# A list scheduler inside the kernel sets every engine's order in a fused window attention and feed-forward kernel, with chunk 1's attention ahead of most weight slices

## The chip, the core and the metric

The kernel runs on one core of a Trainium2 chip. The metric is device time in microseconds (us) of one execution; the kernel before takes 979.98 us, the median of three runs (979.28 to 980.83). The core has five engines that run their own instruction streams in order and wait for each other through semaphores: TensorE (PE; PEld is its weight load), VectorE (DVE), ScalarE (ACT), GpSimd (POOL) and SyncE (SP, which here only issues DMAs).

## What is computed

Windowed causal attention (a query sees itself and the 63 positions before it), then a feed-forward layer with mish, all in float32:

```python
B, H, S, D = 8, 8, 576, 64
scores = q @ k.T / sqrt(D)
mask = (rel >= 0) & (rel < 64)            # rel = query position - key position
attn = exp(scores - max); attn /= sum(attn) + 1e-9
x = (attn @ v).transpose(0, 2, 1, 3).reshape(4608, 512)
h = x @ w_in                               # w_in 512 x 2048
g = h * tanh(log1p(exp(h)))
out = g @ w_out                            # w_out 2048 x 512
```

## The kernel before

The 4608 tokens are cut into 12 chunks (c) of 384. The attention of a chunk is four *units*, one for each pair of heads (p). A unit loads q_t, k_t and v_t; PE makes the scores of six blocks of 64 queries against 128 keys (s_ps, 24 matmuls); DVE reduces each 128x128 piece (L149: adds the mask, gives the row's extreme), ACT takes the exponential (L152), DVE normalises (L156 to L158 in halves for chunk 0, L160 to L162 whole otherwise). The result pr has to be turned: for chunks 0 to 3 PE transposes it into t_ps (L183) and ACT or DVE copies it to pT (L184); for later chunks DVE transposes 32x32 blocks (L172) and twelve small DMAs move them (L177). PE then multiplies with v (o_ps, 24 matmuls), and the sum is split into a high part xh (ACT, L204) and a low part xl (DVE, L205), which only together carry float32.

The feed-forward part runs in *steps* (c, f): 16 slices f of the weights for each chunk. ffn_in makes h_ps from x with 12 matmuls of 128x384 (L213, recorded at helper line L95); ACT applies mish (L220) and the result t is split into gh (ACT for chunk 0, L222; POOL otherwise, L224) and gl (POOL, L225). ffn_out adds nine matmuls of 128x512 into three accumulators acc, two steps later (LAG).

The weights come as 64-bit floats, 1 MB a slice, and load_w turns each slice into a high and a low half once, during the first chunk: ACT clears the sign (L261), DVE does two short operations (L262, L264) and two long ones (L265, L266), ACT rounds (L270), DVE subtracts (L271). The tile wa has two buffers; the load of slice f waits until L266 of slice f-3 is done.

What sets the order: tiles come from pools, and the framework's own scheduler orders each engine's instructions by a simulated time line and priorities (`tc.high_priority`); only from chunk 2 on PE's matmuls are tied into one chain (in_order). The sequence of steps is written out: chunk 0's attention first, the steps (0, f) for f below 8 (HEAD), then (0, f) and (1, f-8) by turns, then the rest of chunk 1, then chunk after chunk. The attention of chunk 1 is planned into the first eight steps (`atts[1].plan`), that of chunk 2 into the last of chunk 1, and every later one over the steps of the chunk before, with four steps between scores and values. The accumulators of chunk 1 use the attention banks (tag "at"), so they can only start when its attention is done.

Of the kernel before, what the change touches and what calls it, by code (L numbers as in the profile page):

```python
# [26 lines left out]
@with_exitstack
def tile_window_attn_mish_ffn(
# [65 lines left out]
    def pe(*args, **kw):
        order.append(nc.tensor.matmul(*args, **kw).ins)  # L95
# [11 lines left out]
    def load_qk(c, p):  # L110
        q_t = ap_.tile([P, CH], F32, name="q_t")
        k_t = ap_.tile([P, CH + BLK], F32, name="k_t", bufs=2)
        parts = NM if c == 0 and p < 1 else 1
        for i in range(parts):
# [4 lines left out]
        return q_t, k_t

    def load_v(c, p):

        v_t = ap_.tile([P, NB, P], F32, name="v_t", bufs=2)
        src = vN[p, c * CH:, :]
        nc.sync.dma_start(v_t, bass.AP(tensor=vN.tensor, offset=src.offset,
                                       ap=[[P, P], [BLK * P, NB], [1, P]]))
        return v_t

    def att_scores(c, p, tiles):
        q_t, k_t = tiles  # L130
        s_ps = [bank(c, p, "s_ps").rearrange("p (m k) -> p m k", k=P) for _ in range(2)]
        pr = ap_.tile([P, HM, P], F32, name="pr", bufs=2)
        mx = ap_.tile([P, HM], F32, name="mx", bufs=3)
        sm = ap_.tile([P, HM], F32, name="sm", bufs=3)
        for m in range(NM):
            for par, h in ((0, 0), (1, 1), (1, 0), (0, 1)):
                n = 2 * m + par
                rows = slice(h * BLK, (h + 1) * BLK)
                pe(s_ps[h][par * BLK:(par + 1) * BLK, m, :],
                   q_t[rows, n * BLK:(n + 1) * BLK], k_t[rows, n * BLK:n * BLK + P],  # L140
                                 start=True, stop=True)
        for h in range(2):
            js = slice(h * NM, (h + 1) * NM)
            for m in range(NM):
                first = [(c * NB + 2 * m + par) % blocks_per_seq == 0 for par in range(2)]
                mk = firsts[first.index(True)] if any(first) else mask
                j = h * NM + m

                nc.vector.tensor_tensor_reduce(  # L149
                    out=pr[:, j, :], in0=s_ps[h][:, m, :], in1=mk,  # L150
                    op0=ALU.add, op1=ALU.min, scale=-0.125, scalar=3.0e38, accum_out=mx[:, j:j + 1])
                nc.scalar.activation(pr[:, j, :], pr[:, j, :], AF.Exp, bias=mx[:, j:j + 1], scale=-1.0,  # L152
                                     accum_out=sm[:, j:j + 1])
            if c == 0:

                nc.vector.tensor_scalar(sm[:, js], sm[:, js], 1e-9, None, ALU.add)  # L156
                nc.vector.reciprocal(sm[:, js], sm[:, js])
                nc.vector.tensor_tensor(pr[:, js, :], pr[:, js, :], sm[:, js].unsqueeze(2).to_broadcast([P, NM, P]), ALU.mult)  # L158
        if c > 0:
            nc.vector.tensor_scalar(sm, sm, 1e-9, None, ALU.add)  # L160
            nc.vector.reciprocal(sm, sm)
            nc.vector.tensor_tensor(pr, pr, sm.unsqueeze(2).to_broadcast([P, HM, P]), ALU.mult)  # L162
        return pr

    def att_transpose(c, p, pr):
        pT = next(pTs)
        if c > 3:


            moved = []  # L170
            tr = ap_.tile([P, P // 32, HM, 32], F32, name="tr", tag="pr", bufs=2)
            nc.vector.transpose(tr.rearrange("p k j i -> p j k i"),  # L172
                                pr.rearrange("p j (k i) -> p j k i", i=32))
            for r in range(0, P, 32):
                for k in range(0, P, 32):
                    if 0 <= k - r % BLK <= BLK:
                        moved.append(nc.sync.dma_start(pT[k:k + 32, r // 32, :, :], tr[r:r + 32, k // 32, :, :]))  # L177
            return pT, moved
        for h in range(2):
            t_ps = (bank(c, p, "t_ps") if c else ps_h.tile([P, CH], F32, name="t_ps", tag="h_ps")  # L180
                    ).rearrange("p (m k) -> p m k", k=P)
            for m in range(NM):
                nc.tensor.transpose(t_ps[:, m, :], pr[:, h * NM + m, :], ident)  # L183
            (nc.scalar.copy if h == 0 or c == 1 else nc.vector.tensor_copy)(  # L184
                pT[:, :, h * NM:(h + 1) * NM, :].rearrange("p r m i -> p m r i"),
                t_ps.rearrange("p m (r i) -> p m r i", i=32))
        return pT, []

    def att_values(c, p, v_t, pT, x):
        pT, moved = pT  # L190
        xh, xl = x
        o_ps = bank(c, p, "o_ps")
        for n in range(NB):
            m, par = n // 2, n % 2
            for h in range(2):
                rows = slice(h * BLK, (h + 1) * BLK)
                pe(o_ps[rows, n * BLK:(n + 1) * BLK], v_t[:, n, rows],
                   pT[:, 2 * par:2 * par + 2, h * NM + m, :], start=True, stop=True)

                for d in moved:  # L200
                    tc.add_manual_dep(order[-1], d.ins.name, SYNC, reason="values in one piece")
                moved = []
        with tc.high_priority(offset=SOON):
            nc.scalar.copy(xh[:, p, :], o_ps)  # L204
            nc.vector.tensor_tensor(xl[:, p, :], o_ps, xh[:, p, :].bitcast(F32), ALU.subtract)  # L205

    def ffn_in(c, x, f):
        xh, xl = x
        h_ps = ps_h.tile([P, CH], F32, name="h_ps", tag="h_ps")
        n = 0  # L210
        for cc in range(NC_):
            for part, xx in ((0, xh), (0, xl), (1, xh)):
                pe(h_ps, ws[f][:, 0, part, cc * P:(cc + 1) * P], xx[:, cc, :],  # L213
                   start=n == 0, stop=n == 3 * NC_ - 1)
                n += 1
        t = mp.tile([P, CH], F32, name="t", tag="t", bufs=4)
        gh = mp.tile([P, CH], F32R, name="gh", bufs=3)
        gl = mp.tile([P, CH], F32R, name="gl", bufs=3)
        with tc.high_priority(offset=SOON):
            nc.scalar.activation(t, h_ps, AF.Mish)  # L220
# [212 lines left out]
```

## Time and profile before

| | |
|---|---|
| median of 3 runs | 979.98 us |
| the profiled execution, its own time | 979.27 us |
| its span, first to last instruction | 977.5 us |
| mean granted TensorE clock | 0.976 |
| start of chunk 2's first step (timeline of PE) | 229.18 us |
| accumulating matmuls from 966.90 us, last of PE | 5.74 us |
| last output store issued (instructions of tile o) | 974.2 us |

The profiled execution is 0.7 us below the median. All times inside it count from the span's start. The granted clock is the share of its full speed that TensorE's clock was given in a stretch. A wait is put down to the engine and line that released it last.

### The profile page before, as it was taken

The numbers are of one execution on the slowest core, as the hardware profiler recorded it, in microseconds if no ns is written. First come the engines' busy times: TensorE is split into PE (matmuls) and PEld (weight loads), VectorE is DVE, ScalarE is ACT, GpSimd is POOL, SyncE is SP. The second block draws the span as 40 slices with busy tenths as digits, with TensorE's granted clock in tenths as the row PEclk, the third lists the DMA queues.
The fourth block names the chain that finished last, engine by engine and source line by source line (L and its number), as shares of the span: only waits on it lengthen the run. The fifth ranks groups of instructions, "written<-read, shape, count | busy, mean of one in ns | idle before, by whom it ended". The sixth has DMA issues, their size and how long they took to land.

```text
span 977.5 us, 16844 instructions
## 1 busy us (share of the span) xinstructions
PE 929.9 (95%) x6432; PEld 821.7 (84%) x6432; DVE 276.3 (28%) x916; ACT 417.8 (43%) x1004; POOL 292.8 (30%) x385
## 2 busy tenths in 40 slices
PE   4698599998999999999999999999999999999998
PEld 2586399887888898888889888898888889889997
DVE  6988800122231321221221221221221221220000
ACT  5689511553553533533533443443443353451111
POOL 1023033231223233333333333333323323323332
PEclk9599699998999999999999999999999999999999
DMA  9655200122121311311311312322222221210000
GB/s 312 229 193 199 95 1 1 50 68 83 52 68 47 113 53 53 113 51 54 112 51 55 110 51 56 101 60 56 90 71 56 85 78 54 84 30 13 33 1 33
DMA packets 78033, 76.09 MB, mean 78 GB/s; under 512 B 9344, under 2 KB 71296, under 8 KB 75904
## 3 DMA queue, kind: packets, MB, share of 16 engines
q1 hardware_dynamic: 77952, 75.01, 24.5%
q8 instruction: 51, 0.84, 0.4%
q14 instruction: 30, 0.25, 0.1%
HBM read 56.10 MB, written 9.44 MB: 67 GB/s over the span
## 4 chain that ended last, share of the span: by engine, by line
PE 87%; DVE 7%; ACT 3%; issue 1%; DMA 1%; SPq 1%; ACTq 0%
PE h_ps L95 40%; PE acc L95 39%; PE o_ps L95 4%; PE s_ps L95 4%; DVE w L271 1%; DVE wa L265 1%; DVE wa L266 1%; DMA st<-w 1%; DVE wa L262 1%; DVE wa L264 1%; ACT wa L261 1%; ACT pr L152 1%; DVE pr L149 1%; PE t_ps L183 1%; ACT L220 1%
## 5 line engine op out<-in xcount | busy, mean ns | idle before, releaser
L95 PE MATMUL h_ps<-xh,w 128*128 128x384 f32 x1536 | 431.1, 341 | 3.7 <-ACT xh L204 2.7
L95 PE MATMUL acc<-w,gh 128*128 128x512 f32 x1152 | 363.5, 397 | 1.5 <-ACT gh L222 1.5
L95 PEld LDWEIGHTS h_ps<-xh,w 128*128 128x128 f32 x1536 | 284.2, 190 | 13.9 <-ACT xh L204 3.3
L220 ACT ACTIVATE t<-h_ps 128x384 f32<-128x384 f32 x192 | 94.0, 491 | 440.4 <-PE h_ps L95 439.7
L95 PE MATMUL h_ps<-xl,w 128*128 128x384 f32 x768 | 260.8, 340 | 2.9 <-DVE xl L205 2.9
L224 POOL TENSOR_SCALAR gh<-t 128x384 fp32r<-128x384 f32 x176 | 90.3, 513 | 568.6 <-ACT t L220 566.1
L95 PEld LDWEIGHTS acc<-w,gh 128*128 128x128 f32 x1152 | 211.9, 188 | 39.7 <-issue 6.3
L225 POOL TENSOR_TENSOR gl<-t,gh 128x384 fp32r<-128x384 f32 x192 | 198.4, 1034 | 106.9 <-ACT gh L222 92.2
L95 PE MATMUL acc<-w,gl 128*128 128x512 f32 x576 | 224.5, 391 | 0.6 <-POOL gl L225 0.6
L95 PEld LDWEIGHTS h_ps<-xl,w 128*128 128x128 f32 x768 | 145.8, 190 | 11.5 <-DVE xl L205 3.9
L205 DVE TENSOR_TENSOR xl<-o_ps,xh 128x384 fp32r<-128x384 f32 x48 | 26.7, 556 | 379.4 <-ACT xh L204 379.4
L95 PEld LDWEIGHTS acc<-w,gl 128*128 128x128 f32 x576 | 108.2, 188 | 25.1 <-POOL gl L225 1.0
L152 ACT ACTIVATE pr<-pr,mx 128x128 f32<-128x128 f32 x288 | 112.1, 391 | 14.8 <-DVE mx L149 14.3
L149 DVE CUSTOM_DVE_ANT_0 pr<-s_ps,mask 128x128 f32<-128x128 f32 x288 | 64.6, 285 | 30.8 <-PE s_ps L95 30.8
L220 ACT ACT_TABLE_LOAD x48 | 61.6, 1283 | 12.7 <-PE h_ps L95 12.4
L152 ACT ACT_TABLE_LOAD x42 | 53.9, 1283 | 28.9 <-DVE mx L149 28.7
L95 PEld LDWEIGHTS o_ps<-pT,v_t 128*64 128x64 f32 x1152 | 43.7, 150 | 24.3 <-issue 11.2
L95 PE MATMUL o_ps<-pT,v_t 128*64 128x64 f32 x1152 | 51.9, 240 | 9.8 <-DVE pT L184 4.7
L95 PE MATMUL s_ps<-k_t,q_t 64*64 64x128 f32 x1152 | 50.8, 293 | 4.0 <-DMA k_t<-kT 4.0
L152 ACT ACTIVATION_READ_ACCUMULATOR pr<-pr,mx 128x1 f32 x288 | 54.0, 187 | 0.0
L243 DVE COPY o<-acc 128x512 f32<-128x512 f32 x12 | 8.3, 692 | 149.2 <-PE acc L95 148.8
L95 PEld LDWEIGHTS s_ps<-k_t,q_t 64*64 64x64 f32 x1152 | 36.1, 140 | 11.3 <-DMA q_t<-qT 3.9
(36 smaller groups left out, 343.9 us busy)
## 6 DMA issues: line engine op xcount, KB each, us to landing
v_t<-vN SPq DMA_DIRECT2D x48, 384.0 KB, 3.7
st<-w SPq DMA_DIRECT2D x16, 1024.0 KB, 5.1
k_t<-kT SPq DMA_DIRECT2D x47, 224.0 KB, 3.8
out<-o SPq DMA_DIRECT2D x36, 256.0 KB, 2.1
pT<-tr SPq DMA_DIRECT2D x384, 24.0 KB, 1.8
q_t<-qT SPq DMA_DIRECT2D x47, 192.0 KB, 3.7
q_t<-qT SPq DMA_DIRECT2D x3, 64.0 KB, 2.0
k_t<-kT SPq DMA_DIRECT2D x2, 64.0 KB, 2.1
```

What stands on the lines that cost most here:

```text
L95: order.append(nc.tensor.matmul(*args, **kw).ins)
L149: nc.vector.tensor_tensor_reduce(out=pr[:, j, :], in0=s_ps[h][:, m, :], in1=mk, op0=ALU.add, op1=ALU.min, scale=-0.125, scalar=3.0e38, acc ...
L152: nc.scalar.activation(pr[:, j, :], pr[:, j, :], AF.Exp, bias=mx[:, j:j + 1], scale=-1.0, accum_out=sm[:, j:j + 1])
L183: nc.tensor.transpose(t_ps[:, m, :], pr[:, h * NM + m, :], ident)
L205: nc.vector.tensor_tensor(xl[:, p, :], o_ps, xh[:, p, :].bitcast(F32), ALU.subtract)
L220: nc.scalar.activation(t, h_ps, AF.Mish)
L224: nc.gpsimd.tensor_scalar(gh, t, 1.0, 0.0, ALU.mult, ALU.add)
L225: nc.gpsimd.tensor_tensor(gl, t, gh.bitcast(F32), ALU.subtract)
L261: nc.scalar.activation(af, hi.bitcast(F32), AF.Abs)
L262: nc.vector.tensor_scalar(af, af, BIG, TINY, ALU.min, ALU.max)
L264: nc.vector.tensor_scalar(a, a, 3, 0x3FFFFFFF, ALU.logical_shift_left, ALU.bitwise_and)
L265: nc.vector.scalar_tensor_tensor(a, hi, 0xC0000000, a, ALU.bitwise_and, ALU.bitwise_or)
```

## The change

The scheduler of the framework is switched off (`tc.manual_schedule()`), and the kernel brings its own. Every piece of work is a Task on one engine with a cost from a table, the buffers that it reads and writes, and a rank. Plan.order walks through time: the engine that can start first takes, among its tasks that are ready at that moment, the one of lowest rank, where an ACT task that needs another function table counts 20 ranks later. The tasks are then emitted sorted by planned start, so each engine's instructions stand in the program in that order. Tiles are fixed rings and the eight PSUM banks are named: A (three, acc), B (three, at), H (two, h).

With it come these moves:

- Ranks: units 0 to 3 have 0 to 6, units 4 to 7 (chunk 1) 22, 32, 34 and 36; slices 0 to 3 have 15, 18, 20 and 30, the later ones 40 to 95. Loads of a slice wait for slice f-2 instead of f-3.
- Chunk 1's steps follow chunk 0's at a distance of five slices (TRAIL) and alternate with them, instead of eight.
- gl of chunks 0 and 1 is made by DVE, gh by ACT; POOL does both from chunk 2 on.
- The sign of slices 6 and up is cleared on DVE instead of ACT.
- Chunk 3 is turned by DVE and DMAs, not by PE.
- Unit 0's q and k are loaded whole, and its k from ACT's queue. Chunk 1's pT copies go both to ACT; of the three stores of a chunk DVE does two.

```diff
+    def order(self):
...
+        for _ in self.tasks:
+            at, e = min((max(free[e], min(r for r, _ in ready[e])), e) for e in ready if ready[e])
+
+            def key(rt):
+                r, t = rt
+                switch = t.table not in (None, table)
+                return t.rank + SWITCH * switch, t.n
+
+            now = [rt for rt in ready[e] if rt[0] <= at + 1e-6]
+            pick = min(now, key=key)
...
+        return sorted(self.tasks, key=lambda t: (t.start, t.n))
...
+    ctx.enter_context(tc.manual_schedule())
...
+        pace = used[f - 2:f - 1] if f > 1 else []
...
+        if on_act:
+            x = add("ACT", "abs", lambda: nc.scalar.activation(af, words[1].bitcast(F32), AF.Abs),
...
+        else:
+            x = add("DVE", "absv", lambda: nc.vector.tensor_scalar(a, words[1], 0x7FFFFFFF, None, ALU.bitwise_and),
...
+        queue = nc.scalar if c == 0 and p == 0 else nc.sync
+        add("SP", "issue", lambda: nc.sync.dma_start(q_t, qT[p, :, a:b]), writes=[u.q[1]], rank=rank, size=P * CH * 4)
+        add("SP", "issue", lambda: queue.dma_start(k_t, kT[p, :, a:b + BLK]), writes=[u.k[1]], rank=rank,
...
+        if c < 2:
+            add("ACT", "gh", lambda: nc.scalar.copy(gh, t), reads=[tb], writes=[ghb], rank=post)
+            add("DVE", "gl", lambda: nc.vector.tensor_tensor(gl, t, gh.bitcast(F32), ALU.subtract),
+                reads=[tb, ghb], writes=[glb], rank=post)
+        else:
+            add("POOL", "poolgh", lambda: nc.gpsimd.tensor_scalar(gh, t, 1.0, 0.0, ALU.mult, ALU.add),
...
+    RANK_U = [0, 2, 4, 6, 22, 32, 34, 36]
+    RANK_W = [15, 18, 20, 30] + [40 + 5 * i for i in range(12)]
...
+    seq = sorted([(f + TRAIL * c + 0.5 * c, c, f) for c in range(2) for f in range(NF)])
+    for n, (_, c, f) in enumerate(seq):
+        ffn_in(c, f, r_ffn(c, f), False, c == 0 and f < 2)
+        if n >= LAG:
+            late(*seq[n - LAG][1:])
...
+            at = (last - NF + 4 * p, last - NF + 4 * p + 4) if c > 3 else (3 + 5 * p // 2, 7 + 5 * p // 2)
```

Three places show what moved. The first is PE around the last two units of chunk 1. Before (xh_557 and xl_558 are chunk 1's, t_ps and o_ps the units'), after the last of chunk 0's steps whose slice is ready:

```order
L183 MATMUL t_ps<-ident,pr 128x128 x6
L95 MATMUL o_ps<-pT_102,v_t 64x64
L95 MATMUL s_ps<-k_t,q_t 64x128 x12
L95 MATMUL o_ps<-pT_102,v_t 64x64 x11
L95 MATMUL h_ps<-xh_557,w 128x384
L95 MATMUL h_ps<-xl_558,w 128x384
L95 MATMUL h_ps<-xh_557,w 128x384
L183 MATMUL t_ps<-ident,pr 128x128 x6
L95 MATMUL o_ps<-pT_103,v_t 64x64 x12
```

In the change (acc_124 to acc_126 are chunk 0's accumulators, the at banks hold the units):

```order
L384 MATMUL at_128<-pT_103,v_t_93 64x64 x12
L348 MATMUL at_129<-ident,pr_96 128x128 x3
L348 MATMUL at_127<-ident,pr_96 128x128 x3
L451 MATMUL acc_124<-w,gh_110 128x512 x2
L451 MATMUL acc_124<-w,gl_113 128x512
L451 MATMUL acc_125<-w,gh_110 128x512 x2
L451 MATMUL acc_125<-w,gl_113 128x512
L451 MATMUL acc_126<-w,gh_110 128x512 x2
L451 MATMUL acc_126<-w,gl_113 128x512
L384 MATMUL at_128<-pT_104,v_t_94 64x64 x12
```

Accumulating matmuls of slice 4 of chunk 0 now stand between the last unit's transposes and its values; before, some eight slices of chunk 0 were ahead of these rows, and nothing but pieces of chunk 1 stood among them.

The second place is DVE while the later slices are made. Before, the operations of two slices (wa has two buffers) follow each other:

```order
L271 TENSOR_TENSOR w<-wa,w 128x2x512
L264 TENSOR_SCALAR wa<-wa 128x1024
L265 SCALAR_TENSOR_TENSOR wa<-st,wa 128x1024
L262 TENSOR_SCALAR wa<-wa 128x1024
L266 SCALAR_TENSOR_TENSOR wa<-st,wa 128x1024
```

In the change (L246 clears the sign, L427 is gl):

```order
L246 TENSOR_SCALAR wa_119<-st 128x1024
L248 TENSOR_SCALAR wa_119<-wa_119 128x1024
L266 TENSOR_TENSOR w<-wa_118,w 128x2x512
L427 TENSOR_TENSOR gl_114<-t_105,gh_111 128x384
L249 TENSOR_SCALAR wa_119<-wa_119 128x1024
L427 TENSOR_TENSOR gl_112<-t_106,gh_109 128x384
L251 SCALAR_TENSOR_TENSOR wa_119<-st,wa_119 128x1024
```

The gl of two steps, which stood on POOL, now stand among the operations of a slice, and one short operation has come over from ACT.

The third place is PE where chunk 2's last unit leads into its first step. Before (acc_1 and acc_2 are chunk 1's accumulators, xh_1681 chunk 2's):

```order
L95 MATMUL acc_2_1110<-w,gh 128x512 x2
L95 MATMUL acc_2_1110<-w,gl 128x512
L95 MATMUL s_ps<-k_t,q_t 64x128 x6
L95 MATMUL o_ps<-pT_102,v_t 64x64 x12
L183 MATMUL t_ps<-ident,pr 128x128 x6
L95 MATMUL o_ps<-pT_103,v_t 64x64 x12
L95 MATMUL h_ps<-xh_1681,w 128x384
```

In the change (at_127 to at_129 are chunk 1's accumulators; the last scores stand just above):

```order
L451 MATMUL at_128<-w,gh_110 128x512 x2
L451 MATMUL at_128<-w,gl_113 128x512
L348 MATMUL acc_125<-ident,pr_95 128x128 x3
L451 MATMUL at_129<-w,gh_110 128x512 x2
L451 MATMUL at_129<-w,gl_113 128x512
L348 MATMUL acc_126<-ident,pr_95 128x128 x3
L384 MATMUL acc_124<-pT_103,v_t_93 64x64 x12
L348 MATMUL acc_125<-ident,pr_96 128x128 x3
L348 MATMUL acc_126<-ident,pr_96 128x128 x3
L384 MATMUL acc_124<-pT_104,v_t_94 64x64 x12
L409 MATMUL h_130<-xh_120,w 128x384
```

Between the last scores and that unit's transposes (pr_96) there stood only the values of the unit before; now nine accumulating matmuls, the transposes and the values of the unit before stand there.

More of the change, by code (lines that the diff above doesn't have):

```diff
@@ L121, in load_v @@
-    def load_v(c, p):
-        v_t = ap_.tile([P, NB, P], F32, name="v_t", bufs=2)
-        src = vN[p, c * CH:, :]
[L125 to L134, printed above, removed]
+    ident = const.tile([P, P], F32, name="ident")
@@ L135, in att_scores, with emit_scores @@
+    class Unit:
+        pass
+    def emit_scores(u):
         for m in range(NM):
@@ L138, in att_scores @@
                 rows = slice(h * BLK, (h + 1) * BLK)
-                pe(s_ps[h][par * BLK:(par + 1) * BLK, m, :],
-                   q_t[rows, n * BLK:(n + 1) * BLK], k_t[rows, n * BLK:n * BLK + P],
+                nc.tensor.matmul(u.s[h][0][par * BLK:(par + 1) * BLK, m * P:(m + 1) * P],
+                                 u.q[0][rows, n * BLK:(n + 1) * BLK], u.k[0][rows, n * BLK:n * BLK + P],
                                  start=True, stop=True)
-        for h in range(2):
[L143 to L178, printed above, removed]
-        for h in range(2):
[L180 to L187, printed above, removed]
@@ new lines, in turn_pe, with tr, copy @@
+    def turn_pe(u, rank, engines, chain):
+        pr, prb = u.pr
+        pr = pr.rearrange("p (j k) -> p j k", k=P)
+        pT, pTb = u.pT = pT_ring.take()
+        for h in range(2):
+            t_ps, tb = u.t[h]
+            def tr(h=h, t_ps=t_ps):
+                for m in range(NM):
+                    nc.tensor.transpose(t_ps[:, m * P:(m + 1) * P], pr[:, h * NM + m, :], ident)
+            add("PE", "tr", tr, reads=[prb], writes=[tb], after=[u.normed[h]], rank=rank, chain=chain)
+            def copy(h=h, t_ps=t_ps):
+                (nc.scalar.copy if engines[h] == "ACT" else nc.vector.tensor_copy)(
+                    pT[:, :, h * NM:(h + 1) * NM, :].rearrange("p r m i -> p m r i"),
+                    t_ps[:, :CH].rearrange("p (m r i) -> p m r i", m=NM, i=32))
+            add(engines[h], "pT", copy, reads=[tb], writes=[pTb], rank=rank)
+        u.moved = []
@@ L196, in att_values @@
                 rows = slice(h * BLK, (h + 1) * BLK)
[L197 to L205, printed above, removed]
@@ L395, in tile_window_attn_mish_ffn, with values @@
-    while pend:
-        with in_order():
-            flush()
+                mm = nc.tensor.matmul(o_ps[rows, n * BLK:(n + 1) * BLK], v_t[:, n, rows],
+                                      pT[:, 2 * par:2 * par + 2, h * NM + m, :], start=True, stop=True)
+                for d in u.moved:
+                    tc.add_manual_dep(mm.ins, d.ins.name, SYNC, reason="values in one piece")
+                u.moved = []
+    def values(u, rank, chain):
+        add("PE", "values", lambda: emit_values(u), reads=[u.v[1], u.pT[1]], writes=[u.o[1]], rank=rank, chain=chain)
@@ new lines, in tile_window_attn_mish_ffn, with bank, tail, front @@
+    rot = [0]
+    def bank(pool):
+        rot[0] += 1
+        return pool[(rot[0] - 1) % 3]
+    def tail(i):
+        u, r = units[i], RANK_U[i]
+        if i >= 4:
+            pool = B if i < 8 else A
+            u.t = [bank(pool), bank(pool)]
+            u.o = bank(pool)
+        turn_pe(u, r, ("ACT", "ACT") if 4 <= i < 8 else ("ACT", "DVE"), False)
+        values(u, r, False)
+        refill_v(i)
+        x_parts(u, r)
+    def front(i):
+        u, r = units[i], RANK_U[i]
+        if i >= 4:
+            pool = B if i < 8 else A
+            u.s = [bank(pool), bank(pool)]
+        scores(u, r, False)
+        refill_qk(i)
+        softmax(u, r, i < 4)
@@ new lines, in tile_window_attn_mish_ffn @@
+    for n, (c, f) in enumerate(steps):
+        r = 1000 + 10 * n
+        ffn_in(c, f, r, True, False)
+        for kind, i in sorted(runs.get(n, []), key=lambda x: x[0], reverse=True):
+            u = units[i]
+            if kind == "s":
+                u.s, u.o = B[:2], B[2]
+                scores(u, r, True)
+                refill_qk(i)
+                softmax(u, r - 4, False)
+                turn_dma(u, r - 4)
+            else:
+                values(u, r, True)
+                refill_v(i)
+                x_parts(u, r - 5)
+        if n >= LAG:
+            ffn_out(*steps[n - LAG], r + 15, True)
@@ L400 @@
+    for n in range(N - LAG, N):
+        ffn_out(*steps[n], 10000 + n, True)
+    tasks = plan.order()
+    if REPORT:
+        REPORT(tasks)
+    for t in tasks:
+        t.emit()
+REPORT = None
 def kernel(**inputs):
```

528 lines of the change are left out of this document (333 added, 195 removed).

## The prediction

> **What bounds the kernel now.** The page first: who is busy.
>
> ```profile
> PE 929.9 (95%) x6432; PEld 821.7 (84%) x6432; DVE 276.3 (28%) x916; ACT 417.8 (43%) x1004; POOL 292.8 (30%) x385
> ```
>
> PE fills the span on average, so the question is where it doesn't. Busy time by stretch (start:end, length, then PE, PEld, DVE, ACT, POOL, each with its count, granted clock, DMA share, GB/s):
>
> ```profile
> 0.00:25.00 25.00, 10.51 (x131) 7.21 (x131) 17.50 (x62) 13.83 (x40) 4.12 (x17) 0.94 0.90 311
> 25.00:50.00 25.00, 17.54 (x133) 13.52 (x133) 24.97 (x62) 16.82 (x43) 0.00 (x0) 0.58 0.69 232
> 50.00:75.00 25.00, 23.04 (x155) 20.03 (x154) 22.15 (x36) 22.13 (x37) 7.12 (x5) 1.00 0.57 202
> 75.00:100.00 25.00, 20.54 (x138) 17.11 (x137) 22.39 (x33) 22.05 (x37) 6.24 (x5) 1.00 0.47 167
> 100.00:125.00 25.00, 13.88 (x102) 10.95 (x103) 19.22 (x35) 13.91 (x28) 2.47 (x3) 0.66 0.29 92
> 125.00:150.00 25.00, 25.00 (x128) 22.78 (x127) 0.00 (x0) 4.48 (x9) 7.62 (x9) 1.00 0.00 1
> ```
>
> Up to 125 us PE is idle for 39.5 us and twice works at a low granted clock (0.58, 0.66), while DVE is busy 106.2 of 125. From 125 on PE is full. What PE waits for before 125 us (total, times, longest):
>
> ```profile
> PE t_ps L183 <- DVE pr L158: 7.7, 3, 3.2
> PE t_ps L183 <- DVE pr L162: 7.0, 3, 3.6
> PE o_ps L95 <- DVE pT L184: 4.7, 2, 2.8
> PE h_ps L95 <- DVE xl L205: 2.9, 3, 1.2
> ```
>
> DVE results, each time: the first 125 us are bound by DVE and by attention chains through it; everything later by PE alone. How much PE has to do at full rate comes from the chain of waits:
>
> ```profile
> 131.54 2.11 PE h_ps L95 x12
> ...
> 148.21 2.11 PE h_ps L95 x12
> ...
> 301.46 2.11 PE h_ps L95 x12
> ...
> 320.01 2.09 PE h_ps L95 x12
> ...
> 966.90 5.74 PE acc L95 x25
> ```
>
> 131.54 to 148.21 is four steps (a slice f for a chunk): 4.167 us each. 301.46 to 320.01 is four steps and one attention unit: 1.88 us a unit. A unit that PE transposes costs 0.60 us more, from one start to the next:
>
> ```profile
> 80.77 0.85 PE L183 MATMUL t_ps<-ident,pr 128*128 128x128 f32 x6 [0.22 <-DVE pr L162]
> 81.37 0.71 PE L95 MATMUL acc<-w,gh 128*128 128x512 f32 x2
> ```
>
> Before: 192 x 4.167 + 48 x 1.88 + 16 x 0.60 = 899.9 us. PE ends at 972.6, so it **loses 72.7 us**, nearly all before 125 us and at chunk 2's start. The change is worth what it cuts from those 72.7, plus 4 x 0.60 (chunk 3 goes to the DMA turn).
>
> **The change, part by part.** *Prices on DVE* (start to next start):
>
> ```profile
> 43.19 0.28 DVE L149 CUSTOM_DVE_ANT_0 pr<-s_ps,mask 128x128 f32<-128x128 f32 x1
> ...
> 43.40 0.29 DVE L149 CUSTOM_DVE_ANT_0 pr<-s_ps,mask 128x128 f32<-128x128 f32 x1
> ...
> 48.54 0.55 DVE L205 TENSOR_TENSOR xl<-o_ps,xh 128x384 fp32r<-128x384 f32 x1
> 49.00 1.22 DVE L266 SCALAR_TENSOR_TENSOR wa<-st,wa 128x1024 uint32<-128x1024 uint32 x1
> 50.14 0.69 DVE L262 TENSOR_SCALAR wa<-wa 128x1024 f32<-128x1024 f32 x1
> 50.74 0.18 DVE L161 RECIPROCAL sm<-sm 128x6 f32<-128x6 f32 x1
> 50.86 0.69 DVE L264 TENSOR_SCALAR wa<-wa 128x1024 uint32<-128x1024 uint32 x1
> 51.47 0.95 DVE L162 TENSOR_TENSOR pr<-pr,sm 128x768 f32<-128x768 f32 x1
> 52.34 1.22 DVE L271 TENSOR_TENSOR w<-wa,w 128x1024 fp32r<-128x1024 f32 x1
> 53.47 2.04 DVE L265 SCALAR_TENSOR_TENSOR wa<-st,wa 128x1024 uint32<-128x1024 uint32 x1
> ```
>
> A softmax reduction 0.21, a 128x384 operation 0.46, a long weight operation 1.14, a short one 0.60, a full norm 0.87; a pair on sm about 0.4 (estimate from two of 0.18). At 53.47 the long one took 2.04: there POOL does its first gl. The change gives the gl of chunks 0 and 1 to DVE: 0.46 more each, but that stretching goes. Not shown before: gl on DVE (taken as the like-sized xl, 0.46; between 0.21 and 1.14) and the sign-clearing on DVE for f of 6 and up (as the short ones, 0.60; same bounds).
>
> *The start.* Unit 0's q and k come whole instead of in three pieces, k by ACT's queue behind the table load. DVE first waits 6.1 us; landings by size:
>
> ```profile
> DVE pr L149 <- PE s_ps L95: 6.1, 1, 6.1
> ```
> ```profile
> st<-w SPq DMA_DIRECT2D x16, 1024.0 KB, 5.1
> ...
> q_t<-qT SPq DMA_DIRECT2D x47, 192.0 KB, 3.7
> ...
> q_t<-qT SPq DMA_DIRECT2D x3, 64.0 KB, 2.0
> ```
>
> 1.7 us later: DVE starts at 7.8. All behind it moves along.
>
> *Chunk 0's attention.* Up to the fourth xl DVE's new order has 26 reductions (5.5), 8 pairs (3.2), 8 half norms (3.7), 4 copies and 4 xl (3.7), and of slices 0 and 1 four short and five long operations (2.4 + 5.7): 24.2 us, so 32.0. DVE's queue is fixed, and its pT copies wait in it for PE's transposes; I add 2: **34 us**. Before, with six slices' work squeezed between, that xl came at 48.54.
>
> *Chunk 1's attention beside slices 2 to 6.* To the last xl of chunk 1: 22 reductions (4.6), 14 short (8.4), 17 long (19.4), 6 gl (2.8), 4 pairs (1.6), 4 norms (3.5), 4 xl (1.8): 42.1, so 76 without a wait. PE's own work there is 6 steps and 4 units, 34.9 us, so DVE leads. ACT must round each slice between two DVE operations, and switches tables nine times; 4 us for that and 2 for PE's steps at low clock: **PE is saturated from 82 us**. Bounds: 76 (no wait) and 90 (DVE waiting 11% as in 50 to 100 us, where it is busy 44.5 of 50, and the first steps slow).
>
> *After that.* Slices 7 to 15 cost DVE 26 long, 24 short, 13 gl: 50 us, 5.6 a slice; PE needs 8.33 for the two steps of one. PE leads. A wait is added here: gl stands in DVE's queue and waits for PE's h and ACT's gh, with the next slice's operations behind it, and SP's slice loads stand behind v loads that wait for PE; the 2.7 us a slice is the cover.
>
> *Into chunk 2.* Before:
>
> ```profile
> 222.21 0.92 PE L95 MATMUL o_ps<-pT,v_t 128*64 128x64 f32 x24
> 226.22 0.85 PE L183 MATMUL t_ps<-ident,pr 128*128 128x128 f32 x6 [3.08 <-DVE pr L162]
> ...
> 229.18 0.69 PE L95 MATMUL h_ps<-xh,w 128*128 128x384 f32 x1
> ```
>
> The last unit's scores ended when o_ps began, so its softmax takes 4.0 us; values covered 0.9, 3.08 were idle. Now nine acc matmuls (4.167 - 2.09, so 2.08), a unit's transposes (0.6) and values (0.9) stand in between: some 0.5 us is left, and short waits at each pT copy. I take 3; bounds 1 and 7 (today's idle twice).
>
> *Steady chunks.* Units again have four steps between scores and values. The twelve moves take SP
>
> ```profile
> 305.13 7.57 SPq L177 DMA_DIRECT2D pT<-tr  x12
> ```
>
> 7.6 us; with softmax 4.0, the turn 1 (sized as the full norm) and a landing 2, about 14.6 of 16.7 us: hidden with 2 us to spare. Other reorderings there cost nothing while PE is full; 1 us for the odd one.
>
> **Sum.** At 82 us PE has done 6 steps and 8 units (44.8). Left: 186 x 4.167 + 40 x 1.88 + 4 x 0.60 = 852.7. 82 + 852.7 + 3 + 1 = 938.7. The tail after PE is today's 977.5 - 972.6 = 4.9; the profiled execution took 1.8 more than its span. **945 us**, against that execution's 979.3, which is 0.7 below the median.
>
> Two rules of the Trainium skill, by themselves. ACT beside a switch:
>
> ```profile
> 66.71 1.15 ACT L261 ACTIVATE wa<-st 128x1024 f32<-128x1024 f32 x1 [1.24 <-DVE w L271]
> 67.88 1.28 ACT L220 ACT_TABLE_LOAD   x1
> 69.17 0.49 ACT L220 ACTIVATE t<-h_ps 128x384 f32<-128x384 f32 x1
> ```
>
> Here a switch costs its 1.28 us and no more. The Trainium skill, "ScalarE: Activation LUTs", section What ACT_TABLE_LOAD costs, adds a drain of about 1.38 us; nine switches in the head would then cost ACT 12 us more and the time would be up to 957 (an estimate); the trace disagrees, so it gets no chance. The Trainium skill, "TensorE: Matmul & The Clock Gate", Part 1, ties half clock to an idle window of about 3.4 us; by it the head, whose waits I put below that, stays at full clock and 2 us fall away. The trace disagrees: 0.58 in 25 to 50 us.
>
> **Rivals.** (a) *The clock stays half until PE is saturated.* From 45 us on PE's remaining 5 steps and 4 units, 30.7 us, become 61: saturated at 106, **969**. For it: 0.58 at a PE share of 70%. Against: 1.00 in 75 to 100 at 82%; I expect 83%.
> (b) *Slices in a closed ring, slower.* DVE's fixed queue makes slice f+1 wait for gl, gl for PE, PE for slice f. Serial, a slice costs h 2.1, ACT's two operations on it 1.0 (0.49 as in the last row above, the second sized alike), gl 0.5, four weight operations 3.5, rounding 1.15 (as the 128x1024 row above), the last long one 1.1, and for chunk 1 again 2.1, 1.0 and 0.5: 13.0 us instead of 8.33. Ten slices lose 47: **992**. It decides from about 11.8 us a slice (34 us over ten). Against: two wa buffers, and today slices overlap at DVE.
> (c) *Units late in the steady chunks.* If SP's moves or ACT's fixed order take more than the 2 us to spare, PE waits at each of 36 units; 1 us each gives **981**, half a microsecond **963**. Against: today's four steps suffice.
> (d) *Fewer waits:* saturated at 76, no loss into chunk 2: **935**.
>
> **How the numbers follow.** Forecast (936 to 957) 0.72; (a) 0.09; (b) 0.05; (c) 0.07, a third of it no gain or slower; (d) 0.07. The range holds the forecast and most of (a) and (c): 935 to 963. A measurement here tells 0.2% from no change. Faster 0.92 (forecast, a, d and two thirds of c); same 0.01 (a sliver of c); slower 0.07 (b and what is left of c).
>
> **What would show it.** Chunk 0's fourth xl near 34 us; PE busy 25 of 25 from about 82; DVE near 50% busy from there to 132, with no 2 us long operations; the step of chunk 2 starting near 200 instead of 229.18; the chain afterwards with 18.5 us per four steps and a unit; no PE wait above 1 us there. The forecast is wrong if PE waits on gl or w after 90 us, or on pT or xl after 210 us.

## Result, and the profile after

| | before | changed kernel |
|---|---|---|
| median | 979.63 us (978.34 to 980.83, 4 runs) | 947.92 us (947.76 to 948.72, 4 runs) |
| ratio to before, 95% interval | | 0.9678 (0.9661 to 0.9695) |
| profiled execution, its span | 979.27, 977.5 | 947.95, 946.2 |
| mean granted TensorE clock | 0.976 | 0.993 |

The kernel is 31.7 us faster; forecast were 34 (945.0, range 935 to 963).

The busy line of the page of the changed kernel:

```profile
PE 918.3 (97%) x6408; PEld 811.2 (86%) x6408; DVE 304.8 (32%) x970; ACT 402.5 (43%) x990; POOL 248.2 (26%) x337
```

Its windows, with the columns as before (PE, PEld, DVE, ACT, POOL, granted clock, DMA share, GB/s):

```profile
0.00:25.00 25.00, 15.98 (x212) 12.12 (x213) 15.37 (x80) 15.46 (x57) 4.22 (x17) 1.00 0.84 262
25.00:50.00 25.00, 19.14 (x114) 15.41 (x112) 22.16 (x50) 20.20 (x37) 0.00 (x0) 0.80 0.54 180
50.00:75.00 25.00, 20.95 (x198) 17.60 (x199) 23.34 (x56) 22.47 (x56) 0.00 (x0) 0.93 0.56 197
75.00:100.00 25.00, 24.48 (x144) 21.86 (x143) 24.40 (x31) 10.25 (x17) 0.00 (x0) 1.00 0.58 196
100.00:125.00 25.00, 25.00 (x127) 22.65 (x126) 24.73 (x31) 10.06 (x16) 0.00 (x0) 1.00 0.46 169
...
175.00:200.00 25.00, 22.52 (x215) 19.12 (x213) 12.97 (x48) 22.35 (x63) 0.00 (x0) 1.00 0.33 102
200.00:225.00 25.00, 23.60 (x180) 21.05 (x181) 6.83 (x26) 11.50 (x25) 8.33 (x12) 1.00 0.21 67
```

PE's idle time up to 125 us fell from 39.5 to 19.5 us. Up to there the clock was lowest at 25 to 50 us (0.58) and at 100 to 125 us (0.66); now it is 0.80 at 25 to 50 us and 0.93 at 50 to 75 us, and 1.00 from there to 125 us. What PE still waits for in the first 90 us, the longest groups (total, times, longest):

```profile
PE acc L295 <- DMA k_t<-kT: 4.4, 1, 4.4
PE at L384 <- ACT pT L353: 3.7, 2, 3.2
PE acc L348 <- ACT w L263: 1.9, 1, 1.9
PE h L409 <- ACT w L263: 1.8, 1, 1.8
PE h L409 <- DVE w L266: 1.6, 3, 0.8
PE acc L451 <- ACT gh L426: 1.4, 1, 1.4
```

The load at the start aside, the largest are now waits for ACT, not for DVE. Added up by what ended them, PE's waits up to 125 us were 22.3 us for DVE, 12.5 for ACT and 4.0 for loads in the kernel before; they are 5.3, 8.8 and 5.3 now. The last gap of the head and the start of chunk 2's first step, from PE's timeline (the value in brackets is the idle time before):

```profile
80.00 0.62 PE L409 MATMUL h<-xh,w 128*128 128x384 f32 x2 [0.52 <-DVE w L266]
...
193.47 0.92 PE L384 MATMUL acc<-pT,v_t 128*64 128x64 f32 x24 [1.83 <-ACT pT L353]
...
199.07 0.91 PE L384 MATMUL acc<-pT,v_t 128*64 128x64 f32 x22 [0.63 <-DVE pT L353]
201.08 0.88 PE L348 MATMUL acc<-ident,pr 128*128 128x128 f32 x6 [1.10 <-DVE pr L327]
202.20 1.32 PE L384 MATMUL acc<-pT,v_t 128*64 128x64 f32 x24 [0.24 <-ACT pT L353]
203.45 0.44 PE L409 MATMUL h<-xh,w 128*128 128x384 f32 x1
```

From 80 to 191 us PE never waits; chunk 2 starts at 203.45 instead of 229.18. The chain of waits gives the rate afterwards:

```profile
756.16 2.11 PE h L409 x12
774.78 2.11 PE h L409 x12
...
871.23 2.10 PE h L409 x12
883.79 2.10 PE h L409 x12
...
936.13 6.18 PE acc L451 x27
```

Four steps and a unit take 18.62 us (18.55 before), and three steps 12.56: **4.187 us a step instead of 4.167**. That is one part in 200, on everything, and no term of the prediction allows for it.

### The profile page after: what moved, and what is told of

It is laid out like the page before. It is cut to its first block, busy times and chain, and to the rows that moved or that the text cites. A ratio compares the mean times of both kernels' runs of the same rounds, so it can differ in the third digit from the quotient of the medians.

```text
span 946.2 us, 16719 instructions
## 1 busy us (share of the span) xinstructions
PE 918.3 (97%) x6408; PEld 811.2 (86%) x6408; DVE 304.8 (32%) x970; ACT 402.5 (43%) x990; POOL 248.2 (26%) x337
## 3 DMA queue, kind: packets, MB, share of 16 engines
q1 hardware_dynamic: 79536, 75.96, 25.8%
## 4 chain that ended last, share of the span: by engine, by line
PE 90%; DVE 5%; ACT 4%; DMA 1%; issue 0%; SPq 0%; ACTq 0%; DVEq 0%
PE h L409 41%; PE acc L451 38%; PE at L384 3%; PE at L295 3%; PE at L451 3%; ACT pr L318 1%; DVE pr L327 1%; DVE w L266 1%; DMA st<-w 1%; DVE wa L251 1%; ACT L318 1%; ACT L424 1%; DMA k_t<-kT 0%; DVE pr L314 0%; DVE wa L256 0%
## 5 line engine op out<-in xcount | busy, mean ns | idle before, releaser
L409 PE MATMUL h<-xh,w 128*128 128x384 f32 x1536 | 427.9, 340 | 3.4 <-ACT w L263 1.8
L409 PEld LDWEIGHTS h<-xh,w 128*128 128x128 f32 x1536 | 282.2, 189 | 13.9 <-DVE w L266 2.9
L424 ACT ACTIVATE t<-h 128x384 f32<-128x384 f32 x192 | 94.2, 491 | 442.0 <-PE h L409 441.5
L409 PE MATMUL h<-xl,w 128*128 128x384 f32 x768 | 259.0, 337 | 0.0
L432 POOL TENSOR_TENSOR gl<-t,gh 128x384 fp32r<-128x384 f32 x160 | 162.0, 1013 | 13.3
L409 PEld LDWEIGHTS h<-xl,w 128*128 128x128 f32 x768 | 145.0, 189 | 7.8
L314 DVE CUSTOM_DVE_ANT_0 pr<-at,mask 128x128 f32<-128x128 f32 x252 | 56.8, 285 | 22.4 <-PE at L295 22.4
L327 DVE TENSOR_TENSOR pr<-pr,sm 128x768 f32<-128x768 f32 (+1 forms) x52 | 46.6, 896 | 1.4
L384 PE MATMUL at<-pT,v_t 128*64 128x64 f32 x984 | 38.6, 226 | 4.6 <-ACT pT L353 3.7
L295 PE MATMUL at<-k_t,q_t 64*64 64x128 f32 x1008 | 40.1, 291 | 0.9 <-DMA k_t<-kT 0.9
```

The lines of the kernel that those rows point to most:

```text
L295: nc.tensor.matmul(u.s[h][0][par * BLK:(par + 1) * BLK, m * P:(m + 1) * P], u.q[0][rows, n * BLK:(n + 1) * BLK], u.k[0][rows, n * BLK:n * ...
L314: x = add("DVE", "ttr", lambda: nc.vector.tensor_tensor_reduce(out=pr[:, j, :], in0=u.s[h][0][:, m * P:(m + 1) * P], in1=mk, op0=ALU.add, ...
L327: return add("DVE", "norm3" if n == NM else "norm6", lambda: nc.vector.tensor_tensor(pr[:, js, :], pr[:, js, :], sm[:, js].unsqueeze(2).to ...
L384: mm = nc.tensor.matmul(o_ps[rows, n * BLK:(n + 1) * BLK], v_t[:, n, rows], pT[:, 2 * par:2 * par + 2, h * NM + m, :], start=True, stop=True)
L409: nc.tensor.matmul(h_ps[:, :CH], ws[f][:, 0, part, cc * P:(cc + 1) * P], xx[:, cc, :], start=cc == 0 and i == 0, stop=cc == NPAIR - 1 and ...
L424: add("ACT", "mish", lambda: nc.scalar.activation(t, h_ps[:, :CH], AF.Mish), reads=[hb], writes=[tb], rank=post, table="mish")
```

## The experiments

All times are medians, all ratios to runs of the kernel before on the same chip. The two faults of the changed kernel that the runs brought out (the address of w and the trail) are told first, since later runs build on them.

| run | us | ratio, 95% interval | change from 947.9 |
|---|---|---|---|
| late_attention | 955.60 | 0.9747 (0.9733 to 0.9760) | +7.7 |
| trail8 | 944.76 | 0.9635 (0.9622 to 0.9648) | -3.2 |
| gl_pool | 958.01 | 0.9760 (0.9738 to 0.9782) | +10.1 |
| turn3_pe | 954.20 | 0.9735 (0.9721 to 0.9749) | +6.3 |
| w_aligned | 944.11 | 0.9632 (0.9619 to 0.9645) | -3.8 |
| trail8_aligned | 940.69 | 0.9596 (0.9583 to 0.9609) | -7.2 |
| gl_pool_trail8 | 948.82 | 0.9671 (0.9657 to 0.9684) | +0.9 |
| turn3_trail8 | 950.64 | 0.9697 (0.9684 to 0.9711) | +2.7 |
| order_alone | 970.60 | 0.9900 (0.9886 to 0.9914) | +22.7 |
| gl_dve_before | 973.74 | 0.9937 (0.9924 to 0.9949) | +25.8 |
| k_by_sp | 947.29 | 0.9670 (0.9656 to 0.9683) | -0.6 |
| sign4 | 938.29 | 0.9587 (0.9571 to 0.9603) | -9.6 |

The runs lie on three chips, where the kernel before took 980.47, 980.45 and 980.17 us, against 979.63 beside the changed kernel. A difference of less than about 1 us between two rows is therefore not to be read, unless the intervals of their ratios are apart.

**The slower step.** Start to start, the twelve matmuls of h take about the same time in both kernels (2.10 us before and 2.11 now, means from 400 to 900 us where accumulating matmuls stand on both sides); the nine accumulating ones take 2.08 instead of 2.06 us. Both use w: for h it is loaded as the weights and x streams through, in the accumulating ones w itself streams. First the chain of the kernel before, then of the changed one:

```profile
713.65 2.10 PE h_ps L95 x12
715.76 2.06 PE acc L95 x9
```
```profile
723.11 2.10 PE h L409 x12
725.21 2.08 PE acc L451 x9
```

Of what differs, the address of w was tried. In the changed kernel it begins 64 bytes past a multiple of 128 in each partition, before at a multiple of 128: the tiles that the changed kernel places ahead of it add up to 81600 bytes, if its six tiles of 24 bytes take 32 each, and those of the kernel before to 8192.

```diff
     wbufs = [Buf() for _ in range(NF)]
+    const.tile([P, 16], F32, name="pad")
```

> The change, with an unused tile of 64 bytes per partition placed ahead of the weights: w then starts at a multiple of 128 bytes in each partition, as before the change; in the changed kernel it starts 64 bytes off. Nothing else differs. Steps took 4.167 us before the change and 4.187 after, all of it in the accumulating matmuls, whose moving operand is w. Theory A (the address of w sets it): steps back at 4.167, 0.020 x some 180 steps = 3.6 us less, 944.3. Rival B (the PSUM banks, which also changed, or the semaphores set it): steps stay at 4.187 and the time at 947 to 949.

The chain of w_aligned:

```profile
719.57 2.08 PE acc L452 x9
721.65 2.09 PE h L410 x12
723.74 2.08 PE acc L452 x9
```

A step is 4.17 us again (719.57 to 723.74), and the whole is 3.8 us shorter. Nothing but the address of w (and of st, which shares its place) differs from the changed kernel, so A holds for the step and the time. It does not hold for the place. The accumulating matmuls still take 2.08 us; what became shorter is h. By the same means, twelve matmuls of h took 2.107 us and take 2.089, and nine accumulating ones took 2.081 and take 2.078, where the kernel before has 2.061. So the expectation was wrong that all of the loss lay in the accumulating matmuls, and what makes those slower than before is not the address of w. It stays open: the banks and the semaphores (B) were not tried for it, nor was the address of x, which is 64 bytes off as well in the changed kernel. That the step comes back to 4.167 us is in part chance: a faster h makes up for what the accumulating matmuls still lose.

**The trail.** The distance between the two chunks' steps, and what remains if chunk 1's attention is late as well:

```diff
-    TRAIL = 5
+    TRAIL = 8
```

> The change, with only the distance between chunk 0's and chunk 1's steps put back from five slices to eight; the attention stays early. Theory A: three slices (5 to 7) are used once instead of twice while DVE makes one in 5.6 us and a step takes 4.19, so 3 x 1.4 = 4.2 us of PE waits on w appear between 80 and 110 us: 952. Rival B: slices are already ahead of PE when it is saturated, so the distance costs nothing: 947 to 949.

Both theories missed: the time fell to 944.8. The windows of trail8, in the stretch where the changed kernel loses 2.48 and 1.40 us of PE:

```profile
75.00:100.00 25.00, 23.84 (x140) 21.00 (x139) 24.24 (x30) 10.61 (x17) 0.00 (x0) 1.00 0.57 192
...
175.00:200.00 25.00, 25.00 (x211) 21.83 (x210) 12.82 (x46) 18.92 (x50) 0.00 (x0) 1.00 0.33 100
200.00:225.00 25.00, 25.00 (x169) 22.52 (x168) 6.46 (x32) 11.92 (x34) 9.19 (x12) 1.00 0.22 73
```

A's waits on w are there, but small: PE is busy 0.64 us less in 75 to 100 us, so slices are further ahead than A counted. What neither theory looked at is the other end of the trail. Chunk 2's attention needs chunk 0's banks, so it can only begin when chunk 0 ends, and it hides behind the steps of chunk 1 that are left, about as many as the trail: five, 20.9 us, don't cover four units that are bound by chains through DVE and ACT; eight, 33.5 us, do. In the changed kernel its first scores start at 169.70 us, and the first step of chunk 2 follows its last values directly, 33.8 us later; in trail8 they start at 157.83, and two groups of chunk 1's accumulating matmuls are still left behind the last values. No PE wait is left between 100 and 300 us.

```diff
-    TRAIL = 5
+    TRAIL = 8
...
-    RANK_U = [0, 2, 4, 6, 22, 32, 34, 36]
+    RANK_U = [0, 2, 4, 6, 100, 120, 140, 160]
...
-    RANK_U += [140 + i for i in range(4)]
+    RANK_U += [240 + i for i in range(4)]
```

(The second pair of ranks is that of chunk 2's units, so that they stay behind chunk 1's.)

> The change, but chunk 1's four units get ranks 100, 120, 140, 160 (behind the first weight slices, beside chunk 0's steps) and chunk 1's steps trail by eight slices, as before the change. Theory A (the gain is the early attention, which gives PE two steps for each slice while DVE still makes slices): slices cost DVE 5.6 us and one step 4.19, so PE waits at every slice until chunk 1 is ready, and the units' DVE chains open waits as before: saturated 8 to 20 us later, 956 to 968. Rival B (the gain is the list order itself, the gl on DVE and no stretched operations; DVE is the bound either way and its total work is the same): within 2 us of the changed kernel, 946 to 950.

955.6, just below A's range and out of B's. The run to compare it with is trail8, which has the same trail: late attention costs 10.8 us. The windows of late_attention show 20.54 and 22.49 where trail8 has 23.84 and 25.00, and a clock below 1.00 in both:

```profile
75.00:100.00 25.00, 20.54 (x129) 15.45 (x128) 24.90 (x46) 22.60 (x38) 0.00 (x0) 0.95 0.60 206
100.00:125.00 25.00, 22.49 (x127) 20.16 (x126) 23.91 (x33) 11.69 (x19) 0.00 (x0) 0.91 0.41 144
```

DVE is as full as in trail8 (24.24 and 24.76 there); it makes the same things in another order. So A's direction holds, B's does not; A's account of waits slice by slice is not shown, since PE waits there for gh, gl, w and the units' chains alike.

trail8 and w_aligned together:

> The change with a trail of eight slices and the 64 bytes ahead of w. If both findings are apart from each other, 944.8 less 3.6: 941.2, with PE full from 100 us on and steps of 4.167. If the address does nothing: 944.8. If the order of trail 8 only won by chance of the clock: 943 to 946.

940.69: the two faults are apart from each other (3.2 and 3.8 make 7.0; measured 7.2, within what these runs can tell).

**gl on POOL.**

```diff
-            add("DVE", "gl", lambda: nc.vector.tensor_tensor(gl, t, gh.bitcast(F32), ALU.subtract),
+            add("POOL", "poolgl", lambda: nc.gpsimd.tensor_tensor(gl, t, gh.bitcast(F32), ALU.subtract),
```

> The change, with the gl of chunks 0 and 1 made by POOL again (gh stays on ACT). Theory A (a gl on POOL stretches a long DVE operation from 1.22 to 2.04 us): the six gl before PE is saturated free 6 x 0.46 = 2.8 us of DVE and cost up to 6 x 0.82 = 4.9 us, so 949 to 951 and long operations of 2 us in the trace. Rival B (no stretching that matters, DVE has 2.8 us less to do): 945 to 947.

958.0, more than A's 951. The timeline of DVE in gl_pool, part of one slice:

```profile
114.26 1.50 DVE L249 TENSOR_SCALAR wa<-wa 128x1024 uint32<-128x1024 uint32 x1
115.80 1.92 DVE L251 SCALAR_TENSOR_TENSOR wa<-st,wa 128x1024 uint32<-128x1024 uint32 x1
117.76 1.23 DVE L256 SCALAR_TENSOR_TENSOR wa<-st,wa 128x1024 uint32<-128x1024 uint32 x1
```

Short operations are held up like long ones (1.50 instead of 0.69, 1.92 instead of 1.22; POOL makes two gl from 114.03 to 116.65 us), in both chunks, up to the last slice, where A counted only six before 82 us. The Trainium skill, "SBUF — State Buffer", section SBUF: two separate sides, has GpSimd and some of DVE's operations lock a shared pair of ports for a whole instruction; these rows agree.

> Trail of eight and gl of chunks 0 and 1 on POOL. With a trail of five POOL's gl cost 10 us, of which the windows put 4.8 before 150 us and the rest at chunk 2's start, with one half-clock stretch. Theory A (stretching: each gl on POOL adds 0.82 us to a DVE operation and takes 0.46 off DVE, so DVE makes slices later; the loss at chunk 2's start was the trail's): 944.8 + 5 = 950, with no waits after 150 us. Rival B (POOL's longer latency for gl costs at chunk 2's start whatever the trail): 954 to 956.

948.8, so 4.1 us for gl on POOL, and no waits at chunk 2's start but one of 0.5 us: the number is A's. A's account is not. DVE's busy time from 25 to 150 us, first of trail8, then of gl_pool_trail8:

```profile
25.00:150.00 125.00, 103.97 (x178) 0.93 0.43 147
```
```profile
25.00:150.00 125.00, 104.69 (x155) 0.93 0.43 147
```

DVE has as much to do with gl on POOL as without: its stretched operations cost it 11 us more there (0.5 us a gl, not the 0.82 that A took), and 23 gl of 0.55 us, 12.7 us, fell away. What grows is DVE's idle time, by 4.0 us from 25 to 75 us; from 25 to 82 us DVE waits 7.1 us for ACT instead of 3.7. The list scheduler makes another order for every engine when gl changes its engine, and whether that order or the stretching makes DVE wait was not tried apart.

The other 6 us of gl_pool went with the trail of five, where the lateness grows: in the profiles chunk 2's first scores come 7.7 us later than in the changed kernel (177.40 and 169.70) and its first step 10.5 us (213.99 and 203.45), while with a trail of eight these come 5.8 and 5.9 us later than in trail8. Where its chunk 2 starts the clock of gl_pool was 0.86.

The same part done alone in the kernel before:

```diff
-            nc.gpsimd.tensor_tensor(gl, t, gh.bitcast(F32), ALU.subtract)
+            (nc.vector if c < 2 else nc.gpsimd).tensor_tensor(gl, t, gh.bitcast(F32), ALU.subtract)
```

> The kernel before, with only the gl of chunks 0 and 1 moved from POOL to DVE; all else and the framework's scheduler as they were. Theory A (a gl on POOL adds 0.82 us to a DVE operation, on DVE it costs 0.46, and DVE is the bound up to 125 us): about 20 of them there, 20 x 0.36 = 7 us: 971 to 976. Rival B (DVE has spare time around them, or the gl wait in its queue): 979 to 984.

973.7, in A's range: 6.4 us. By the clock the two kernels differ too. It is recorded as 1.00 at 25 to 50 us (0.58 before) and as 0.55 at 100 to 125 (0.66 before), as the windows of gl_dve_before show:

```profile
25.00:50.00 25.00, 15.61 (x133) 11.62 (x133) 24.97 (x62) 16.84 (x44) 0.00 (x0) 1.00 0.67 233
...
100.00:125.00 25.00, 15.59 (x69) 12.53 (x68) 18.70 (x29) 11.89 (x26) 1.02 (x2) 0.55 0.25 87
```

The first of these is not the edit's doing. The first gl of the kernel before starts at 52.38 us, and from 25 to 40 us PE's rows are the same in both kernels to within 0.15 us, the slow matmuls among them; only the clock that is recorded for them differs. How the 6.4 us divide between DVE's time and the clock behind 50 us stays open.

**Chunk 3's turn.**

```diff
+                if u.c == 3:
+                    u.t = B[:2]
+                else:
+                    turn_dma(u, r - 4)
...
+                if u.c == 3:
+                    turn_pe(u, r - 4, ("ACT", "DVE"), True)
                 values(u, r, True)
```

> The change, with chunk 3 turned by PE again instead of by DVE and DMAs. Theory A: PE is full in chunk 2, so each of four units adds its 0.60 us of transposes: 2.4 us, 950.3, and with a wait for the pT copies up to 1 us a unit more. Rival B: the DMA turn was itself what delayed the start of the steady part (waits of chunk 3's units between 200 and 250 us), so the time is the same or shorter: 946 to 948.

> Trail of eight and chunk 3 turned by PE. With a trail of five that turn cost 6.3 us: 2.4 by the transposes as priced, the rest by waits for pT and one half-clock stretch at chunk 2's start. Theory A (the rest belongs to the trail's gaps at chunk 2's start): 944.8 + 2.4 = 947.2, up to 948.5 with short waits at each of the four units. Rival B (each unit turned by PE waits for its pT copy and costs 1.5 us): 950 to 952.

Both +6: 6.3 at a trail of five, 5.9 at eight, so B of the second holds, that the units themselves pay, and its A falls. PE's waits of turn3_trail8 from 160 to 300 us (its windows lose the same 2.8 us between 225 and 275 us):

```profile
PE at L384 <- ACT pT L353: 2.8, 4, 1.7
```

2.4 for the transposes and 2.8 for four waits make 5.2; the rest, 0.7, is not explained. The waits come from where this list puts transposes and values, one behind the other in PE's chain, with nothing between them but the copy of pT.

**The order alone.** The scheduler, rings and banks stay, and so do unit 0's loads and DVE's two stores of a chunk; the other parts go back (chunk 1's pT copies were ACT's in the kernel before too):

```diff
-    TRAIL = 5
+    TRAIL = 8
...
-        pace = used[f - 2:f - 1] if f > 1 else []
+        pace = used[f - 3:f - 2] if f > 2 else []
...
-        if c < 2:
+        if c < 1:
             add("ACT", "gh", lambda: nc.scalar.copy(gh, t), reads=[tb], writes=[ghb], rank=post)
...
-    RANK_U = [0, 2, 4, 6, 22, 32, 34, 36]
+    RANK_U = [0, 2, 4, 6, 100, 120, 140, 160]
...
-    ACT_ABS = 6
+    ACT_ABS = NF
```

and with these chunk 2's ranks as in late_attention, and w_aligned's, gl_pool's and turn3_pe's edits.

> The list scheduler, its fixed tiles and banks and the address of w as before the change, with the other parts put back: chunk 1's attention late, trail eight, gl of chunks 0 and 1 and gh of chunk 1 on POOL, all sign clearing on ACT, chunk 3 turned by PE, slice loads paced by three. Theory A (the parts add up, and the list order has a worth of its own): 955.6 - 3.6 (address) + 4.1 (gl) + 5.9 (turn) = 962, and 0 to 5 for the other two, 960 to 967. Rival B (the order alone is worth nothing; the parts carry the whole gain and only overlap): 976 to 981.

970.6, between the two. The order alone, with what stays beside it, is worth 9.6 us, and the parts do not add: from here to trail8_aligned are 29.9 us, while late attention, gl and turn one by one make 20.8 (10.8, 4.1 and 5.9); gh of chunk 1, sign clearing and pacing were not tried apart. The window of order_alone in which PE is idle most, and two of PE's waits from 50 to 130 us:

```profile
100.00:125.00 25.00, 14.34 (x91) 11.64 (x90) 20.12 (x26) 18.35 (x39) 0.00 (x0) 0.66 0.18 59
```
```profile
PE at L349 <- DVE pr L328: 5.6, 2, 4.7
PE h L410 <- DVE w L267: 5.4, 4, 2.0
```

This is the kernel before again (13.88 busy, clock 0.66): chunk 0's steps are used up, chunk 1's last units are in DVE, PE idles and the clock is low. That several of the parts act on this hole, and that this makes up the 9 us that don't add, is likely, not shown.

**The start.**

```diff
-        queue = nc.scalar if c == 0 and p == 0 else nc.sync
+        queue = nc.sync
```

> The change, with unit 0's k issued by SP behind its q instead of by ACT. Theory A (ACT issues a DMA beside its table load): k is issued some 0.5 us later than at 0.76, the first reduction starts at 6.5 to 6.9 instead of 6.14, and the time is 0 to 0.7 us longer, 947.9 to 948.6. Rival B (as the prediction had it, the issue on ACT comes behind the load): the first reduction starts at 4.8 to 6.1 and the time is shorter.

The first reduction came at 5.61 us instead of 6.14, the time did not change measurably. First the issues of the changed kernel, then of k_by_sp:

```profile
0.73 1.28 ACT L177 ACT_TABLE_LOAD   x1 [0.73 <-PEq L633]
0.74 0.39 SPq L275 DMA_DIRECT2D q_t<-qT  x1
0.76 0.40 ACTq L276 DMA_DIRECT2D k_t<-kT  x1
...
4.42 1.56 PE L295 MATMUL acc<-k_t,q_t 64*64 64x128 f32 x24 [4.42 <-DMA k_t<-kT]
...
6.14 0.29 DVE L314 CUSTOM_DVE_ANT_0 pr<-acc,mask 128x128 f32<-128x128 f32 x1 [6.14 <-PE acc L295]
```
```profile
1.18 0.42 SPq L276 DMA_DIRECT2D k_t<-kT  x1
...
3.89 1.56 PE L295 MATMUL acc<-k_t,q_t 64*64 64x128 f32 x24 [3.89 <-DMA k_t<-kT]
...
5.61 0.29 DVE L314 CUSTOM_DVE_ANT_0 pr<-acc,mask 128x128 f32<-128x128 f32 x1 [5.61 <-PE acc L295]
```

ACT's issue is recorded beside its table load, yet PE can use the data only 3.66 us later, SP's 2.71 us after its issue. By the DMA packets of the traces, k's first packet starts at 2.61 us in the changed kernel, 1.85 us after the issue, and at 2.43 in k_by_sp, 1.25 after; and q, which SP issues at 0.74 us in both, also comes later, its last packet starting at 3.58 instead of 2.72. B had the earlier reduction right and A that the issue stands beside the load; the shorter time of B isn't shown. Whether the table load, ACT's queue or the v load that SP issues at 1.18 us beside them makes both loads late stays open.

**A further step.** On top of trail8_aligned:

```diff
-    ACT_ABS = 6
+    ACT_ABS = 4
...
-SWITCH = 20.0
+SWITCH = 40.0
```

> The 940.7 us version (trail eight, 64 bytes ahead of w), with the sign of slices 4 and 5 cleared on DVE too and table switches counted as 40 ranks instead of 20. Theory A (ACT's queue with its switches makes PE's waits on pT, w and gh before 80 us): two operations of 1.15 us and the switches around them leave ACT for 1.2 us on DVE; PE saturated 1 to 3 us earlier, 938 to 940. Rival B (DVE is the bound before 80 us): 1 us later, 941 to 943.

938.3 against 940.7, but the intervals of the two ratios overlap (0.9571 to 0.9603, 0.9583 to 0.9609), so the step isn't shown. In its windows PE is busy 25.00 of 25 us from 75 to 100 us, where trail8_aligned has 23.09, but 24.25 from 225 to 250, where that has 25.00.

## Why the prediction was right

The mechanism was the forecast's: PE is the bound once it is full, and the change is worth the time by which it is full sooner. One reading that it began with was too narrow. "DVE results, each time" rests on four rows of PE's waits, 22.3 us; the same list has 12.5 us for ACT and 4.0 for loads, two of its rows being

```profile
PE o_ps L95 <- ACT pT L184: 4.4, 4, 2.3
PE s_ps L95 <- DMA k_t<-kT: 4.0, 3, 3.5
```

and ACT's waits are those of which most is left. Point by point:

- **The start**, charged with 1.7 us, cost nothing: DVE began at 6.14 us, against 6.08 before. The charge compared one whole load (3.7 us) with one piece (2.0), but before, the pieces were issued one behind the other, the last at 3.07 us, and DVE waited for the scores of all three. They began at 3.52 us and ended at 5.92, with waits between; in the change they begin at 4.42 and end at 5.98 without one.
- **Fourth xl of chunk 0**: 32.47 against 34, which is the 1.7 again. The 26.2 us for work and waits came to 26.3, by luck in part: behind its start DVE waited 3.3 us instead of 2, so its work was about 23.0 instead of 24.2.
- **PE full**: from 80 us instead of 82.
- **DVE afterwards**: forecast near half load from 82 to 132 us, which does not fit its own 50 us of work; it is full to 125, and its last operation on a slice ends at 134.9. The total was right, the pacing by PE was wrong: none of DVE's waits from 80 to 150 us is put down to PE. It cost nothing.
- **The rate**: the step's 4.167 was taken as a constant of the work, and became 4.187. This is **the term that was mis-sized**; w_aligned, with steps of 4.167, takes 3.8 us less.
- **Into chunk 2**: 3.8 us of waits at 193 to 203 us, forecast 3, and one for the odd wait (0.7 at 244 us). The bounds 1 and 7 held, but the cause was only half seen: that five left-over steps are too few follows from the trail, and in trail8 these waits are gone.
- **Chunk 3's turn**: priced at 2.4 us, worth 5.9 in this order.
- **The tail**: 3.9 us (946.2 - 942.31), forecast 4.9.

The sum comes out, with errors of both signs that partly offset each other: unrounded the forecast was 945.4. PE is full 2 us sooner; from there to its end pass 862.3 us instead of 856.7, 5.6 more, of which the 186 steps still to do explain 3.7 (0.02 each) and, as far as the rows tell, waits and units at chunk 2's start the rest; the tail is 1.0 shorter. 945.4 - 2 + 5.6 - 1.0 = 948.0, and the profiled execution took 947.95.

Of the rivals none came. (a) The clock: below 1.00 only before 75 us. (b) The closed ring: no PE wait from 80 to 191 us. (c) Late units in the steady chunks: none after 250 us. (d) Fewer waits: 80 us lies between the forecast and it.

The two rules of the Trainium skill: the drain of "ScalarE: Activation LUTs", section What ACT_TABLE_LOAD costs, is again not in the trace: in the changed kernel a table load starts at 58.66 us and takes 1.28, and the next operation of ACT starts at 59.96. The idle window of "TensorE: Matmul & The Clock Gate", Part 1, read as one wait of that length, does not fit either: the clock is 0.80 in 25 to 50 us, where no wait of PE is longer than 1.9 us.

## What to carry to other kernels

When two consumers of one producer are staggered, look at both ends: the distance that feeds the front must leave enough work to cover what starts at the back. A rate that everything runs at is a term like any other, so measure it again after each change of layout; here 64 bytes of padding were worth as much as the choice of the trail. And when an edit brings a rate back, look which part of it came back: the pad restored the step, but not the matmuls that it was meant for. Undo parts beside the best version, not beside the changed one: at the trail of five gl seemed to cost 10.1 us, of which 6 went with the trail.

## What was not expected of the hardware

- Where w begins in each partition sets part of a step's time. At 64 bytes past a multiple of 128 a step takes 4.187 us, in all traces of kernels without the pad on the new layout; with 64 bytes of padding it takes 4.167. The rows put the difference into the matmuls of h, for which w is loaded as the weights (2.107 and 2.089 us for twelve), and hardly into the accumulating ones, through which it streams (2.081 and 2.078 us for nine). Why was not tried, nor why the latter took 2.061 us in the kernel before.
- The half clock does not follow from the waits alone: before chunk 2's first step the changed kernel and turn3_pe have the same waits (1.83, 0.63, 1.10 and 0.24 us), and only turn3_pe fell to a clock of 0.86 in 200 to 225 us. There the last two groups of the unit, six transposes and 22 of the values, took 1.54 us each, where the changed kernel needs 0.88 for the transposes and 1.32 for 24 of the values. Each is one execution, so this is a difference between executions and not shown to be one between kernels.
- The first load issued by ACT could be used 3.66 us after its issue, the same 224 KB issued by SP after 2.71.
